# Channel mixing in pairs of feature blocks, with two PSUM banks read by one instruction

## The chip, the core and the metric

The kernel runs on one NeuronCore of a Trainium2 chip. Five engines with queues of their own work on it: TensorE (PE in the profile, its weight loads PEld), VectorE (DVE), ScalarE (ACT), GpSimd (POOL) and SyncE (SP). Each takes its instructions strictly in the order in which they were issued to it; an instruction that waits for a semaphore holds up all that stand behind it on its engine.

The metric is the time of one execution on the device in microseconds. Before the change the median of three runs is 2263.96 us.

## The reference

Eight batches of 4096 tokens with 192 channels go through an attention over seven taps and then through two matrix products over tokens and two over channels.

```python
# attention: a causal window of K = 7 rows, weights by head (8 heads of 24 channels)
w = softmax(weight_gen)                      # B, S, H, K
out = einsum('bshk,bskhg->bshg', w, x_unf)   # x_unf: the window's rows
# token mixing, d_tok = 256
h = maximum(xt @ w_tok1, 0) @ w_tok2         # xt: channels by tokens
u = x + h.T
# channel mixing, d_ch = 1536
h2 = maximum(u @ w_ch1, 0) @ w_ch2
result = u + h2
```

The products are to be as good as float32. [...]

## The kernel before

**Chunks and blocks.** A batch is cut into 8 chunks of 512 tokens, 64 chunks in all. The 1536 features of the channel mixing are 12 blocks of 128. The main loop (line 811) goes over the chunks `g` and within each over the blocks `f`. One step is `channel1(g, f)`, five matmuls of 512 columns into one PSUM bank `ph` (line 504), and behind it `channel2` for the block two before (`LAG = 2`): eight matmuls, four of 384 columns (line 520) and four of 192 (line 522), which add up in the four banks `acc`.

**From `ph` to `h`.** When a `ph` is complete, ScalarE writes `relu(ph)`, rounded, as the hi part of `h` (line 507), and after that VectorE writes `relu(ph) - hi` as the lo part (line 508). Only then may the bank be written again. `ph` has a ring of two banks, `ps_h`, so that block `f + 2` waits on TensorE for the lo part of block `f`.

**Between the blocks.** Three kinds of work for other chunks stand between the steps of a chunk. `token1` (eight matmuls of 384 and eight of 192 columns into `th`, lines 397 and 398) is the first token product of a chunk up to nine chunks ahead; VectorE adds what it leaves to `h1s` (lines 406 and 408). `token2_half`, called twice, is the second token product of chunk `g + 1` (into `up`, lines 452 and 453); ScalarE copies its right-hand part to `q2` (line 461), VectorE adds the left-hand part to the attention's result (line 463) and later `q2` to that (line 472). `th` and `up` share a ring of their own, one tile of two banks (`ps_m`). [...]

**The columns of the next chunk.** `channel1` of chunk `g + 1` needs `u` with the channels on the partitions, in two parts. `columns_of` makes them once both halves of `token2` are done: VectorE transposes blocks of 32 by 32 (line 476, tile `t`), ScalarE moves 24 pieces of 32x128 to their partitions (line 484, tiles `a_f` and `c_f`), then it casts `a_hi` and the upper half of `uc` (lines 424 and 425), and VectorE takes the differences `a_lo` and the lower half of `uc` (lines 426 and 429). The first matmul of a step reads `a_hi`, the third `a_lo`, the fourth and the fifth `uc`.

**Attention.** VectorE computes the taps of a chunk eight to nine chunks ahead: seven multiplications (line 200) and six additions (line 208) of 128x768.

**Who sets the order.** The program is written by a planner in Python that runs when the kernel is built. It keeps an estimated time per engine (`at`), adds a cost for what it issues, and lets `pump(limit)` put waiting work (the attention, conversions, column moves) between the steps as long as VectorE would not be later than `limit`, which is `SLACK` past the time at which the next lo part can be taken. A column move is planned at 200 ns. On the chip only the resulting order is in force; the engines wait for semaphores, not for the plan.

**Leaving a chunk.** `store` (line 526) adds `acc` and `u`: VectorE the left-hand parts (line 534), ScalarE copies the right-hand parts to `q` (line 535), VectorE adds them (line 539), and GpSimd's queue issues the store (line 540).

**Stages.** Up to 130 us the first batch's attention and token mixing are done and the weights are converted. The token products take float32 values in the first two batches and split ones from the third on. In the last batch there is no attention and no `token1` left.

Of the kernel before, what the change touches and what calls it, by code (L numbers as in the profile page):

```python
# [21 lines left out]
def mixer_kernel(ctx: ExitStack, tc: tile.TileContext, x, wg, wt1, wt2, wc1, wc2, out):  # L22
# [11 lines left out]
    NF = F // P  # L34
    KR = R // P
# [34 lines left out]
    xt = {}  # L70

    def load_x(m):
        """Four rows on each partition, with the six rows before them."""
# [72 lines left out]
    def split(hi, lo, v):  # L146
        """The part of v that TensorE takes in one pass, and the rest."""
# [28 lines left out]
    def taps(src, wn, j, k0, k1):  # L176
        """The rows of taps k0..k1-1, and their weights along the channels of a head."""
# [38 lines left out]
    def two_parts(m):  # L216
        """For the token mixing, after the first batches."""
# [13 lines left out]
    # The first batch, before anything is there for TensorE to do: it adds up the taps.  # L231
# [35 lines left out]
    def load_w1(m):  # L267
        """The first batches take float32 values; for the next one they are split, once."""
# [40 lines left out]
    def load_w2(m):  # L309
        """The first batches take float32 values; for the next one they are split, once."""  # L310
# [122 lines left out]
    Q = 32                   # VectorE transposes blocks of so many rows and columns  # L433
    NQ = P // Q
    ur, q2 = {}, {}

    def token2_half(m, half):
        """Two of the four tokens of each partition."""
        b, i = divmod(m, NCH)
        xa, h1, w = xat[m], h1t[b], w2t[m]  # L440
        if m == 0 and half == 1:
            up = ps_acc.tile([P, 2, 512], F32, tag="acc0", name="up")
        else:
            up = ps_m.tile([P, 2, 512], F32, tag="m", name="up")
# [22 lines left out]
    def columns_of(m):  # L467
        """The same with the channels on the partitions: the blocks transposed, then each moved."""
        box = {}

        def add():
            nc.vector.tensor_add(ur[m], ur[m], q2.pop(m))

        def turn():
            t = late.tile([P, CT, D], F32, tag="q2", name="t")
# [10 lines left out]
        if m in q2:  # L486
            yield "v", 876, add
# [8 lines left out]
    ht, acc_t = {}, {}  # L496

    def channel1(g, f):
        a_hi, a_lo, uc = ut[g]
        ph = ps_h.tile([P, N], F32, tag="ph", name="ph")  # L500
        fs = slice(f * P, (f + 1) * P)
        steps = ((w1a_hi, a_hi), (w1a_lo, a_hi), (w1a_hi, a_lo), (w1c_hi, uc), (w1c_lo, uc))
        for n, (w, u) in enumerate(steps):
            nc.tensor.matmul(ph, w[:, fs], u, start=n == 0, stop=n == len(steps) - 1)  # L504
# [7 lines left out]
    def channel2(g, f):  # L512
# [10 lines left out]
        if f == NF - 1:  # L523
            ut.pop(g)
# [364 lines left out]
```

## Time and profile before

| | |
|---|---|
| median of three runs (lowest to highest) | 2263.96 us (2263.43 to 2265.24) |
| span of the profiled execution | 2262.6 us |
| instructions | 31755 |
| PE busy | 2173.1 us, 96% |
| DVE busy | 1846.8 us, 82% |
| ACT busy | 1253.6 us, 55% |
| POOL busy | 58.5 us, 3% |
| HBM traffic over the span | 107 GB/s |

The span runs from the first instruction to the last. Busy times are unions of an engine's instructions. A matmul's duration in the trace reaches past the start of the next one, because matmuls are pipelined; what TensorE really takes for one is read from start to start. The same holds, by a smaller amount, for VectorE. The profiled execution's span lies 1.4 us under the median of the runs.

### The profile page before, as it was taken

To read this page: it belongs to the slowest core of one execution; us is meant where nothing else is said; L and a number is where in the kernel's file an instruction comes from. 1 tells how busy PE (TensorE), PEld (TensorE's weight loads), DVE (VectorE), ACT (ScalarE), POOL (GpSimd) and SP (SyncE) were. 2 spreads that over 40 slices of the span, in tenths; PEclk is the share of its full clock that TensorE was granted. 3 is DMA by queue.
4 is the path that set the end of the run, shared out by engine and by line. 5 is a ranking of instruction groups with operands and counts; after the bars stand their busy time and mean duration, and the time that the engine had idled before them with its cause. 6 is when DMAs were issued, how large, how long until landed. Compare 5 with 4: busy or idle time off the path is not lost.

```text
span 2262.6 us, 31755 instructions
## 1 busy us (share of the span) xinstructions
PE 2173.1 (96%) x12256; PEld 1946.5 (86%) x12256; DVE 1846.8 (82%) x2504; ACT 1253.6 (55%) x2873; POOL 58.5 (3%) x104
## 2 busy tenths in 40 slices
PE   7969999999999999999999999999999999999997
PEld 5658889999889889889888888888888898888987
DVE  8978889999888889788888888888888888644443
ACT  4686553655565555555556455555545555555553
POOL 0000000000000000000000000000000000000000
PEclk9989999999999999999999999999999999999999
DMA  7734122333323333223323322322332331111100
GB/s 277 244 131 146 65 100 82 121 128 116 111 113 124 117 123 137 102 92 128 110 84 124 128 95 99 128 105 85 128 128 87 107 124 70 64 52 52 52 33 15
DMA packets 52136, 244.75 MB, mean 108 GB/s; under 512 B 6008, under 2 KB 15736, under 8 KB 38672
## 3 DMA queue, kind: packets, MB, share of 16 engines
q1 hardware_dynamic: 43360, 196.58, 24.8%
q0 software_dynamic: 8624, 46.14, 5.0%
q8 instruction: 96, 1.57, 0.3%
q14 instruction: 56, 0.46, 0.1%
HBM read 192.36 MB, written 50.33 MB: 107 GB/s over the span
## 4 chain that ended last, share of the span: by engine, by line
PE 36%; issue 31%; ACT 18%; DVE 13%; DMA 1%; POOL 1%; SPq 0%; POOLq 0%; ACTq 0%; DVEq 0%
PE ph L504 15%; ACT a_f L484 8%; PE acc L520 8%; ACT h L507 4%; PE acc L522 4%; ACT c_f L484 3%; DVE h L508 3%; PE th L397 2%; PE up L452 2%; PE tapsum L251 2%; PE up L450 2%; DVE pr L200 2%; DVE xa L208 2%; PE th L398 1%; DVE prk L240 1%
## 5 line engine op out<-in xcount | busy, mean ns | idle before, releaser
L520 PE MATMUL acc<-w2s,h 128*128 128x384 f32 x3072 | 914.1, 354 | 2.8 <-ACT q L535 2.7
L507 ACT ACTIVATE h<-ph 128x512 fp32r<-128x512 f32 x768 | 458.0, 597 | 661.5 <-PE ph L504 616.4
L522 PE MATMUL acc<-w2s,h 128*128 128x192 f32 x3072 | 770.4, 251 | 0.0
L508 DVE SCALAR_TENSOR_TENSOR h<-ph,h 128x512 fp32r<-128x512 f32 x768 | 527.2, 686 | 297.3 <-ACT h L507 293.6
L522 PEld LDWEIGHTS acc<-w2s,h 128*128 128x128 f32 x3072 | 584.8, 190 | 29.8
L520 PEld LDWEIGHTS acc<-w2s,h 128*128 128x128 f32 x3072 | 577.0, 188 | 37.3 <-ACT q L535 4.8
L504 PE MATMUL ph<-a_hi,w1a_hi 128*128 128x512 f32 x768 | 333.2, 434 | 49.2 <-DVE h L508 38.9
L208 DVE TENSOR_TENSOR xa<-xa,pr 128x768 f32<-128x768 f32 x336 | 319.2, 950 | 0.3
L200 DVE TENSOR_TENSOR pr<-xt,wn 128x768 f32<-128x768 f32 x336 | 317.1, 950 | 2.4
L484 ACT COPY a_f<-t 32x128 f32<-32x128 f32 x1024 | 302.7, 296 | 17.6 <-DVE t L476 5.2
L504 PE MATMUL ph<-uc,w1c_hi 128*128 128x512 f32 x768 | 302.5, 394 | 2.2 <-DVE uc L429 2.2
L504 PE MATMUL ph<-a_lo,w1a_hi 128*128 128x512 f32 x768 | 303.8, 396 | 0.0
L504 PE MATMUL ph<-a_hi,w1a_lo 128*128 128x512 f32 x768 | 302.6, 394 | 0.0
L504 PE MATMUL ph<-uc,w1c_lo 128*128 128x512 f32 x768 | 299.0, 389 | 0.0
L504 PEld LDWEIGHTS ph<-a_hi,w1a_hi 128*128 128x128 f32 x768 | 144.5, 188 | 72.7 <-DVE h L508 61.0
L504 PEld LDWEIGHTS ph<-uc,w1c_hi 128*128 128x128 f32 x768 | 144.5, 188 | 36.6 <-DVE uc L429 3.2
L504 PEld LDWEIGHTS ph<-uc,w1c_lo 128*128 128x128 f32 x768 | 144.6, 188 | 34.2
L504 PEld LDWEIGHTS ph<-a_lo,w1a_hi 128*128 128x128 f32 x768 | 144.6, 188 | 32.9 <-DVE a_lo L426 0.8
L484 ACT COPY c_f<-t 32x128 f32<-32x128 f32 x512 | 152.2, 297 | 7.1
L504 PEld LDWEIGHTS ph<-a_hi,w1a_lo 128*128 128x128 f32 x768 | 147.0, 191 | 0.1
L452 PE MATMUL up<-h,w 128*128 128x384 f32 x384 | 118.4, 364 | 3.6 <-PE acc L522 3.1
L397 PE MATMUL th<-xh,w 128*128 128x384 f32 x384 | 112.9, 359 | 0.0
(72 smaller groups left out, 2026.1 us busy)
## 6 DMA issues: line engine op xcount, KB each, us to landing
w<-s SPq DMA_DIRECT2D x80, 1024.0 KB
xt<-in_x_dram SPq DMA_DIRECT2D x56, 960.0 KB
out_dram<-o POOLq DMA_DIRECT2D x63, 384.0 KB, 3.1
raw<-in_moe_w_tok_dram SPq DMA_DIRECT2D x16, 1024.0 KB
s<-w POOLq DMA_DIRECT2D x16, 1024.0 KB, 4.2
val<-s SPq DMA_DIRECT2D x24, 512.0 KB
wg<-in_weight_gen_dram SPq DMA_DIRECT2D x64, 112.0 KB
s<-val SPq DMA_DIRECT2D x8, 512.0 KB
```

The source lines that it names most:

```text
L200: nc.vector.tensor_mul(dst.rearrange("p t (h g) -> p (t h) g", h=H).rearrange("p (o n) g -> p o n g", o=1), x_k, w)
L208: nc.vector.tensor_add(box["acc"], box["acc"], box.pop(k))
L251: nc.tensor.matmul(ps[:, n, 0:half * D], ident, prs[k][:, n * half:(n + 1) * half, :], start=k == 0, stop=k == K - 1)
L397: nc.tensor.matmul(th[:, r, 0:2 * D], w[:, c, 0, rs], xh[:, c, :], start=c == 0, stop=False)
L450: nc.tensor.matmul(up[:, j, 0:D], w[:, k, cs], h1[:, k, :], start=k == 0, stop=k == KR - 1)
L452: nc.tensor.matmul(up[:, j, 0:2 * D], w[:, k, 0, cs], h1[:, k, :], start=k == 0, stop=False)
L484: nc.scalar.copy(dst[to:to + Q, :].rearrange("p (c n j) -> p c n j", c=CT, n=NQ)[:, :, n, :], box["t"][n * Q:(n + 1) * Q, :, d, :])
L504: nc.tensor.matmul(ph, w[:, fs], u, start=n == 0, stop=n == len(steps) - 1)
L507: nc.scalar.activation(h[:, 0], ph, AF.Relu)
L508: nc.vector.scalar_tensor_tensor(h[:, 1], ph, 0.0, h[:, 0].bitcast(F32), op0=ALU.max, op1=ALU.subtract)
L520: nc.tensor.matmul(ps[:, 0:2 * D], h[:, 0, cs], w2s[:, f, :], start=f == 0, stop=False, **kw)
L522: nc.tensor.matmul(ps[:, 0:D], h[:, 1, cs], w2s[:, f, 0:D], start=False, stop=f == NF - 1, **kw)
```

## The change

- The 12 blocks of a chunk become 6 pairs (`NP`). `channel1(g, p)` runs the ten matmuls of two blocks into a tile of two banks; one instruction of ScalarE and one of VectorE then read both banks (128x2x512 elements) for the hi and the lo parts. `h` holds a pair and has three buffers instead of four single ones.
- `channel2(g, p)` takes a pair, sixteen matmuls, and runs two pairs behind.
- `ps_h` and `ps_m` are replaced by `ps_w`: two tiles of two banks each, which pairs and token products take in turn, in the order of the program.
- The right-hand parts of `up` and of `acc` are no longer copied by ScalarE: VectorE adds them from PSUM, each with one more instruction. `store` adds into `ur` (three buffers) and stores from there; `o`, `q` and `q2` go.
- The planner's costs and rules follow: `C1, C2 = 2290, 2264` for the two products of a pair, `TOP, LOW = 1040, 1135` for the two reads, `LATE = 300`, `FIRST = 0`, one queue `w_at` for the times at which the two tiles come free. The cost of a column move stays 200.

```diff
-    ps_h = ctx.enter_context(tc.tile_pool(name="ps_h", bufs=2, space=bass.MemoryType.PSUM))
-    ps_m = ctx.enter_context(tc.tile_pool(name="ps_m", bufs=1, space=bass.MemoryType.PSUM))
+    ps_w = ctx.enter_context(tc.tile_pool(name="ps_w", bufs=2, space=bass.MemoryType.PSUM))
...
-        th = ps_m.tile([P, 2, 512], F32, tag="m", name="th")
+        th = ps_w.tile([P, 2, 512], F32, tag="w", name="th")
...
+        up = ps_w.tile([P, 2, 512], F32, tag="w", name="up")
...
-            ur[m] = late.tile([P, CT, D], F32, tag="ur", name="ur", bufs=2)
+            ur[m] = late.tile([P, CT, D], F32, tag="ur", name="ur", bufs=3)
+        u = ur[m][:, ts, :]
+        nc.vector.tensor_add(u, up[:, :, 0:D], xa[:, ts, :])
         if b >= F2:
-            if half == 0:
-                q2[m] = late.tile([P, CT, D], F32, tag="q2", name="q2")
-            nc.scalar.copy(q2[m][:, ts, :], up[:, :, D:2 * D])
-        yield
-        nc.vector.tensor_add(ur[m][:, ts, :], up[:, :, 0:D], xa[:, ts, :])
+            nc.vector.tensor_add(u, up[:, :, D:2 * D], u)
...
-    def channel1(g, f):
+    def channel1(g, p):
         a_hi, a_lo, uc = ut[g]
-        ph = ps_h.tile([P, N], F32, tag="ph", name="ph")
-        fs = slice(f * P, (f + 1) * P)
+        ph = ps_w.tile([P, 2, 512], F32, tag="w", name="ph")
         steps = ((w1a_hi, a_hi), (w1a_lo, a_hi), (w1a_hi, a_lo), (w1c_hi, uc), (w1c_lo, uc))
-        for n, (w, u) in enumerate(steps):
-            nc.tensor.matmul(ph, w[:, fs], u, start=n == 0, stop=n == len(steps) - 1)
-        h = late.tile([P, 2, N], F32R, tag="h", name="h", bufs=4)
-        ht[g, f] = h
-        nc.scalar.activation(h[:, 0], ph, AF.Relu)
+        for j in range(2):
+            fs = slice((2 * p + j) * P, (2 * p + j + 1) * P)
+            for n, (w, u) in enumerate(steps):
+                nc.tensor.matmul(ph[:, j, :], w[:, fs], u, start=n == 0, stop=n == len(steps) - 1)
+        h = late.tile([P, 2, 2, N], F32R, tag="h", name="h", bufs=3)
+        ht[g, p] = h
+        nc.scalar.activation(h[:, :, 0, :], ph, AF.Relu)
         nc.vector.scalar_tensor_tensor(
-            h[:, 1], ph, 0.0, h[:, 0].bitcast(F32), op0=ALU.max, op1=ALU.subtract
+            h[:, :, 1, :], ph, 0.0, h[:, :, 0, :].bitcast(F32), op0=ALU.max, op1=ALU.subtract
         )
...
     def store(g):
...
-        for n in range(2):
-            nc.vector.tensor_add(o[:, ts[n], :], a[n][:, :, 0:D], u[:, ts[n], :])
-            nc.scalar.copy(q[:, ts[1 - n], :], a[1 - n][:, :, D:2 * D])
...
+        for n, a in enumerate(acc_t.pop(g)):
+            t = slice(2 * n, 2 * n + 2)
+            for l in range(2):
+                nc.vector.tensor_add(u[:, t, :], a[:, :, l * D:(l + 1) * D], u[:, t, :])
...
-    LATE = 200               # ScalarE for the copies of h
-    FIRST = 1                # the block of features from which on the next chunk's token mixing may come
-    h_at, ph_at, h1_at = {}, [0.0, 0.0], {0: 0.0}
+    LATE = 300
+    FIRST = 0
+    C1, C2 = 2290, 2264
+    TOP, LOW = 1040, 1135
+    h_at, w_at, h1_at = {}, deque([0.0, 0.0]), {0: 0.0}
...
-                    end = max(at["pe"], ph_at[0]) + 1080 + LATE
+                    end = max(at["pe"], w_at[0]) + C1 + LATE
```

**How the order moves.** Before, a chunk in the middle of the run is on TensorE: blocks 0 and 1, `token1`, block 2, the first half of `token2`, block 3, the second half, blocks 4 to 11. After, it is pair 0, first half, pair 1, `token1`, pair 2, second half, pairs 3, 4 and 5. Each block or pair stands here for both its products.

On ScalarE, the columns of the next chunk in the middle of a chunk before, from the reads of blocks 4 and 5 (line 507 is the hi part, line 484 a column move):

```order
L507 ACTIVATE h<-ph 128x512 x2
L484 COPY a_f<-t 32x4x32 x8
L507 ACTIVATE h<-ph 128x512
L484 COPY a_f<-t 32x4x32 x8
L507 ACTIVATE h<-ph 128x512
L484 COPY c_f<-t 32x4x32 x8
L507 ACTIVATE h<-ph 128x512
L424 CAST a_hi<-a_f 128x512
L425 CAST uc<-c_f 64x512
L507 ACTIVATE h<-ph 128x512 x5
```

The same place after, from the reads of pairs 2 and 3 (line 499 is the hi part of a pair, line 476 a column move):

```order
L499 ACTIVATE h<-ph 128x2x512 x2
L476 COPY a_f<-t 32x4x32 x16
L476 COPY c_f<-t 32x4x32 x2
L499 ACTIVATE h<-ph 128x2x512
L476 COPY c_f<-t 32x4x32 x6
L424 CAST a_hi<-a_f 128x512
L425 CAST uc<-c_f 64x512
L499 ACTIVATE h<-ph 128x2x512 x3
```

Where eight moves stood between two reads, eighteen stand now, and six more with both casts behind the read of pair 4.

On VectorE, the end of a chunk before, from the lo part of block 8 to that of block 11 (line 508; `a_lo` and `uc` are the next chunk's):

```order
L508 SCALAR_TENSOR_TENSOR h<-ph,h 128x512
L426 TENSOR_TENSOR a_lo<-a_f,a_hi 128x512
L200 TENSOR_TENSOR pr<-xt,wn 128x768
L429 TENSOR_TENSOR uc<-c_f,uc 64x512
L508 SCALAR_TENSOR_TENSOR h<-ph,h 128x512
L208 TENSOR_TENSOR xa<-xa,pr 128x768
L508 SCALAR_TENSOR_TENSOR h<-ph,h 128x512
L200 TENSOR_TENSOR pr<-xt,wn 128x768
L208 TENSOR_TENSOR xa<-xa,pr 128x768
L508 SCALAR_TENSOR_TENSOR h<-ph,h 128x512
```

After, from the lo part of pair 4 (line 500) over that of pair 5 to that of pair 0 of the next chunk:

```order
L500 SCALAR_TENSOR_TENSOR h<-ph,h 128x2x512
L200 TENSOR_TENSOR pr<-xt,wn 128x768
L426 TENSOR_TENSOR a_lo<-a_f,a_hi 128x512
L208 TENSOR_TENSOR xa<-xa,pr 128x768
L429 TENSOR_TENSOR uc<-c_f,uc 64x512
L500 SCALAR_TENSOR_TENSOR h<-ph,h 128x2x512
L200 TENSOR_TENSOR pr<-xt,wn 128x768
L208 TENSOR_TENSOR xa<-xa,pr 128x768
L200 TENSOR_TENSOR pr<-xt,wn 128x768
L208 TENSOR_TENSOR xa<-xa,pr 128x768
L500 SCALAR_TENSOR_TENSOR h<-ph,h 128x2x512
```

Up to four instructions of 128x768 or smaller stand between two lo parts now, where one to two stood.

Chunk 5 and the last chunks of the second to the sixth batch (15, 23, 31, 39 and 47) now carry two `token1`, behind pairs 0 and 1, and the halves of `token2` behind pairs 2 and 3. The chunks 16, 24, 32, 40 and 48 carry no `token1` and have the halves behind pairs 0 and 1, as the chunks from 56 on have.

More of the change, by code (lines that the diff above doesn't have):

```diff
@@ L34, in mixer_kernel @@
     NF = F // P
+    NP = NF // 2
     KR = R // P
@@ L469, in columns_of @@
         box = {}
-        def add():
-            nc.vector.tensor_add(ur[m], ur[m], q2.pop(m))
         def turn():
-            t = late.tile([P, CT, D], F32, tag="q2", name="t")
+            t = late.tile([P, CT, D], F32, tag="t", name="t")
             nc.vector.transpose(t.rearrange("p c d -> p (c d)"), ur[m].rearrange("p c d -> p (c d)"))
@@ L555, in mixer_kernel @@
     SLACK_M = 400
-    LATE = 200
-    FIRST = 1
-    h_at, ph_at, h1_at = {}, [0.0, 0.0], {0: 0.0}
-    free = {"acc": 0.0, "m": 0.0, "u": 0.0}
+    LATE = 300
[3 more added lines that the diff above has]
+    h_at, w_at, h1_at = {}, deque([0.0, 0.0]), {0: 0.0}
+    free = {"acc": 0.0, "u": 0.0}
     ready = deque()
@@ L776, in do_token1 @@
         next(it)
-        end = on("pe", 2160 if m >= F1 * NCH else 2600, t, free["m"])
+        end = on("pe", 2264 if m >= F1 * NCH else 2600, t, w_at.popleft())
         state["token1"] = m
@@ L780, in do_token1 @@
         next(it, None)
-        free["m"] = on("dve", 1000 if m >= F1 * NCH else 500, end)
+        w_at.append(on("dve", 1000 if m >= F1 * NCH else 500, end))
         if m % NCH == NCH - 1:
-            h1_at[m // NCH] = on("act", 420, free["m"])
+            h1_at[m // NCH] = on("act", 420, w_at[-1])
             if m >= F2 * NCH:
@@ L813, in mixer_kernel @@
         state["rush"] = g == 0
-        for f in range(NF if g < NG else LAG):
+        for p in range(NP if g < NG else LAG):
             if g == 0:
-                need(lambda: f * P < HF or ("w1a", 1) in done)
-            if g == 0 and f >= LAG:
-                need(lambda: ("c2", (f - LAG) // NF2) in done)
+                need(lambda: (2 * p + 2) * P <= HF or ("w1a", 1) in done)
+            if g == 0 and p >= LAG:
+                need(lambda: ("c2", 2 * (p - LAG) // NF2) in done)
             if g < NG:
-                channel1(g, f)
-                end = on("pe", 1080, ph_at.pop(0), free["u"] if f == 0 else 0.0)
-                end = on("act", 480, end)
-                h_at[g, f] = on("dve", 602, end)
-                ph_at.append(h_at[g, f])
-            n = g * NF + f - LAG
+                channel1(g, p)
+                end = on("pe", C1, w_at.popleft(), free["u"] if p == 0 else 0.0)
+                end = on("act", TOP, end)
+                h_at[g, p] = on("dve", LOW, end)
+                w_at.append(h_at[g, p])
+            n = g * NP + p - LAG
             if n >= 0:
-                prev = divmod(n, NF)
+                prev = divmod(n, NP)
                 channel2(*prev)
-                on("pe", 1080, h_at.pop(prev))
-                if prev[1] == 0:
-                    on("pe", 0, free["acc"])
-            if f == LAG - 1 and g > 0:
-                items = store(g - 1)
-                item = next(items)
-                end = on("act", 740, at["pe"] + HOP)
-                free["acc"] = max(end, on("dve", 940, at["pe"] + HOP))
-                chains.append(Chain(chain([item], items)))
+                on("pe", C2, h_at.pop(prev), free["acc"] if prev[1] == 0 else 0.0)
+            if p == LAG - 1 and g > 0:
+                store(g - 1)
+                free["acc"] = on("dve", 2000, at["pe"] + HOP) - 570
             pump(next_lo() + (SLACK if g > NCH else SLACK0))
-            if token1_ready() and (f == LAG - 1 or ready[0][0] < g + NCH + ((g + 1) % NCH == 0)):
+            if token1_ready() and (p == LAG - 1 or ready[0][0] < g + NCH + ((g + 1) % NCH == 0)):
                 do_token1()
@@ L842, in mixer_kernel @@
                 next(parts, None)
-            elif f >= FIRST and g + 1 in w2t and (g + 1) // NCH in h1t \
-                    and max(free["m"], h1_at[(g + 1) // NCH]) <= at["pe"]:
+            elif p >= FIRST and g + 1 in w2t and (g + 1) // NCH in h1t \
+                    and max(w_at[0], h1_at[(g + 1) // NCH]) <= at["pe"]:
                 parts = do_token2(g + 1)
```

58 lines of the change are left out of this document (22 added, 36 removed).

## The prediction

> **What bounds the kernel now.** I read the page first (shares, slices, groups), then the waits, then a table of windows cut where chunks begin, then the timelines of TensorE, ScalarE and VectorE around one chunk. The table holds `channel1`'s matmuls (line 504) alone; 60 of them are a chunk, 480 are eight. Its first columns are the window, its length and TensorE's busy time.
>
> ```profile
> PE 2173.1 (96%) x12256; PEld 1946.5 (86%) x12256; DVE 1846.8 (82%) x2504; ACT 1253.6 (55%) x2873; POOL 58.5 (3%) x104
> 170.90:413.10 242.20, 116.09 (x421) 1.00 0.29 102
> 413.10:679.30 266.20, 131.04 (x480) 1.00 0.31 116
> 679.30:950.50 271.20, 130.97 (x480) 0.99 0.33 118
> 950.50:1215.00 264.50, 129.37 (x480) 1.00 0.30 109
> 1215.00:1479.80 264.80, 129.35 (x480) 1.00 0.31 109
> 1479.80:1744.70 264.90, 129.31 (x480) 1.00 0.30 109
> 1744.70:2008.80 264.10, 129.37 (x480) 1.00 0.25 88
> 2008.80:2221.20 212.40, 112.75 (x421) 1.00 0.12 44
> ```
>
> A chunk takes 33.1 us in the middle and 30.3 in the last batch. What TensorE would need without waits comes from starts (block, `token1`, block, half of `token2`, block):
>
> ```profile
> 1515.42 0.41 PE L504 MATMUL ph<-a_hi,w1a_hi 128*128 128x512 f32 x1
> 1516.59 0.33 PE L520 MATMUL acc<-w2s,h 128*128 128x384 f32 x1
> 1517.70 0.36 PE L397 MATMUL th<-xh,w 128*128 128x384 f32 x1
> 1519.98 0.42 PE L504 MATMUL ph<-a_hi,w1a_hi 128*128 128x512 f32 x1
> 1522.25 0.36 PE L452 MATMUL up<-h,w 128*128 128x384 f32 x1
> 1523.39 0.41 PE L504 MATMUL ph<-a_hi,w1a_hi 128*128 128x512 f32 x1
> ```
>
> A block takes 1.17 + 1.11 = 2.28 us, `token1` 2.28, a half 1.14. Twelve blocks and the token products make 31.92. So a middle chunk loses 1.1 us, and 48 chunks from 413.1 to 2008.8 lose 1595.7 - 48 x 31.92 = 63.5. The waits say to what: TensorE stands before a new `ph` until VectorE has taken the lo part, and never long for the next chunk's columns.
>
> ```profile
> PEld ph L504 <- DVE h L508: 61.0, 96, 6.6
> 1507.03 0.69 DVE L508 SCALAR_TENSOR_TENSOR h<-ph,h 128x512 fp32r<-128x512 f32 x1 [0.68 <-ACT h L507]
> 1507.78 0.50 PE L504 MATMUL ph<-a_hi,w1a_hi 128*128 128x512 f32 x1 [0.38 <-DVE h L508]
> 1508.11 0.40 PE L504 MATMUL ph<-a_hi,w1a_lo 128*128 128x512 f32 x1
> ```
>
> TensorE starts 0.06 us after the lo part ends, and its first step after a wait takes 0.33 instead of 0.25. VectorE had itself waited for ScalarE, which is late because of column moves:
>
> ```profile
> 1516.79 0.60 ACT L507 ACTIVATE h<-ph 128x512 fp32r<-128x512 f32 x1 [1.69 <-PE ph L504]
> 1533.49 0.60 ACT L507 ACTIVATE h<-ph 128x512 fp32r<-128x512 f32 x1
> 1534.11 2.44 ACT L484 COPY a_f<-t 32x128 f32<-32x128 f32 x8
> 1539.69 0.60 ACT L507 ACTIVATE h<-ph 128x512 fp32r<-128x512 f32 x1
> 1540.31 0.62 ACT L424 CAST a_hi<-a_f 128x512 fp32r<-128x512 f32 x1
> 1540.84 0.61 ACT L425 CAST uc<-c_f 64x512 fp32r<-64x512 f32 x1
> ```
>
> ScalarE reads 0.20 after TensorE turns to the next product (1516.59, 1516.79). Eight moves take 2.47 with the gap behind them, 0.309 each, where the plan counts 0.20. A move follows a read by 0.62.
>
> **The change part by part.** TensorE's work stays: the same matmuls in another order.
>
> *The two wide reads.* Nothing before reads 1024 elements of PSUM; these rows bound it:
>
> ```profile
> L507 ACT ACTIVATE h<-ph 128x512 fp32r<-128x512 f32 x768 | 458.0, 597 | 661.5 <-PE ph L504 616.4 <-DVE h L508 37.4 <-DVE xa L208 3.4
> L508 DVE SCALAR_TENSOR_TENSOR h<-ph,h 128x512 fp32r<-128x512 f32 x768 | 527.2, 686 | 297.3 <-ACT h L507 293.6
> L424 ACT CAST a_hi<-a_f 128x512 fp32r<-128x512 f32 x64 | 39.7, 620 | 1.5
> L426 DVE TENSOR_TENSOR a_lo<-a_f,a_hi 128x512 fp32r<-128x512 f32 x64 | 44.1, 688 | 2.8 <-ACT a_hi L424 2.8
> L149 ACT CAST w<-val 128x1024 fp32r<-128x1024 f32 x16 | 16.7, 1045 | 0.2
> L150 DVE TENSOR_TENSOR w<-val,w 128x1024 fp32r<-128x1024 f32 x16 | 19.4, 1213 | 1.1 <-ACT w L149 1.1
> L476 DVE STREAM_TRANSPOSE t<-ur 128x768 f32<-128x768 f32 x64 | 62.1, 971 | 0.5
> ```
>
> From 512 to 1024 elements a cast grows by 425 ns and a difference by 525. So I take 597 + 450 = 1.05 us for the hi part (1.0 to 1.19, twice the narrow one) and 686 + 530 = 1.22 for the lo part (1.15 to 1.37). The tile is free 0.20 + 1.05 + 0.03 + 1.22 + 0.06 = 2.56 us after the pair's last matmul at best.
>
> VectorE is busy 82% and idles 297 us before line 508, all for ScalarE; ScalarE is busy 55%. Neither is saturated. [...]
>
> *The copies that go to VectorE.* Per chunk four copies of 128x384 leave ScalarE. VectorE gets eight additions of 128x384 for four such and two of 128x768: the same elements in two more instructions. A narrow lo part holds VectorE 0.61 (below), 0.53 of it for its 512 elements, so each costs some 0.1. It hides where VectorE idles; without that cover it is 0.2 a chunk, inside the bounds below.
>
> *The ring.* Order on TensorE after: pair 0, half, pair 1, `token1`, pair 2, half, pairs 3, 4, 5. Two tiles are taken in turn, so pair 1 takes pair 0's tile after only one second product and a half, 2.22 + 1.14 = 3.36 us; against 2.56 that leaves 0.8. Pair 3 takes pair 2's on the same terms; the others have 4.5 to 6.8.
>
> *The columns.* Set 0 where the second half's matmuls end. Before, eight blocks followed to the next chunk, 18.2 us; now three pairs, 13.68. Nothing gets shorter for it: still 24 moves, now with 18 in one run ahead of pair 4's read. VectorE's rows:
>
> ```profile
> 1048.77 0.95 DVE L208 TENSOR_TENSOR xa<-xa,pr 128x768 f32<-128x768 f32 x1
> 1049.76 0.96 DVE L200 TENSOR_TENSOR pr<-xt,wn 128x768 f32<-128x768 f32 x1
> 1050.63 0.68 DVE L508 SCALAR_TENSOR_TENSOR h<-ph,h 128x512 fp32r<-128x512 f32 x1
> 1540.96 0.69 DVE L426 TENSOR_TENSOR a_lo<-a_f,a_hi 128x512 fp32r<-128x512 f32 x1
> 1541.57 0.95 DVE L200 TENSOR_TENSOR pr<-xt,wn 128x768 f32<-128x768 f32 x1
> 1542.56 0.69 DVE L429 TENSOR_TENSOR uc<-c_f,uc 64x512 fp32r<-64x512 f32 x1
> 1543.27 0.69 DVE L508 SCALAR_TENSOR_TENSOR h<-ph,h 128x512 fp32r<-128x512 f32 x1
> 1543.88 0.95 DVE L208 TENSOR_TENSOR xa<-xa,pr 128x768 f32<-128x768 f32 x1
> ```
>
> From start to start: `xa` to `pr` 0.99, `pr` to the next 0.87 (I take that for `xa` to a lo part too), `a_lo` 0.61, an attention instruction to `uc` 0.99, `uc` 0.71, a lo part 0.61, so a wide one 0.61 + 0.53 = 1.13.
>
> ScalarE: read of pair 3 at 2.34 + 0.20 = 2.54; moves from 2.54 + 0.62 + 0.45 = 3.61 (two additions and the transpose, at most 0.2 + 0.87 + 0.87 + 0.97, are done by then); 18 x 0.309 later, at 9.17, the read of pair 4, whose matmuls were done at 6.90; six moves from 10.24; `a_hi` 12.09 to 12.71, `uc` to 13.23; read of pair 5.
>
> VectorE: lo of pair 4 at 9.17 + 1.05 + 0.03 = 10.25; `pr` 11.38; `a_lo` waits for `a_hi`, 12.74; `xa` 13.35; `uc` 14.34 to 15.03; lo of pair 5 at 15.05; `pr`, `xa`, `pr`, `xa` from 16.18; lo of the next pair 0 at 19.78 to 21.00; pair 1 may start at 21.06.
>
> TensorE: the next pair 0 at 13.68; its fourth matmul, 0.70 later, waits for `uc` until 15.09, 0.7 lost. Pair 1 would come at 13.68 + 4.56 + 1.14 = 19.38 without waits. It comes at 21.06: **1.7 us lost per regular chunk**. The rest of the chunk fits: counted from pair 1's start, VectorE is through its lo part at 4.8, `store`'s four additions at 6.9, `token1`'s two and a difference of 128x768 at 9.1 (some 2 more with a softmax); the lo part of pair 2 ends at 11.8 to 12.4, and pair 3 is due at 12.6. Period 33.6.
>
> *Batch ends.* Where the halves stand behind pairs 2 and 3, two pairs are left, 9.12 us. `a_hi` is done at 12.71, so pair 0 waits 3.65, then `uc` until 15.09 costs 1.54, with the restart 5.3. Before, such chunks lost no more than others: the rows of all four late batches lie at 264.1 to 264.9. The chunk after has its halves behind pairs 0 and 1, but its moves behind pair 3: chain and end both lie a pair later, and an `Exp` of some 0.5 stands in the chain, so the chunk that follows it loses 1.7 + 0.5 = 2.2. The double `token1` chunk itself loses 0.7 + 0.1 alone, because `token1` stands between its pairs 0 and 1.
>
> *The sum* from 413.1 to 2008.8: 32 regular chunks x 1.7 = 54.4; five batch ends x 5.3 = 26.5; five x 2.2 = 11; six x 0.8 = 4.8; 96.7 together. Of the 63.5 lost before, 8 stay: the second and third batch's rows are 1.7 and 6.5 above their neighbours, for float32 products and the splitting of weights. So 96.7 - 55.5 = +41. In the last batch pair 1 follows at 3.36 without attention in VectorE's queue, and columns have four pairs, 18.2: no waits, 6 x 4.56 + 2.28 = 29.64 against 212.4 / 7 = 30.34, -5 in seven chunks. Chunks 1 to 7 lose 11 of their 242.2 to conversions; I leave that at 0 (one early batch end against smoother pairs, -8 to +8). The span becomes 2262.6 + 41 - 5 = 2298.6. The runs' median lies 1.4 above the span: **2300**.
>
> Both wide reads at their cheap ends shorten the chain by some 0.3 on ScalarE and 0.3 on VectorE: 32 x 0.6 + 5 x 0.5 = 22 less, 2278. At the dear ends (+0.28 and +0.45): 27 more, 2327.
>
> **The rivals.** *Faster.* The chain from the second half to pair 1 is short enough and pairs remove the waits. It decides at 19.38: the chain must lose 1.7 of 21.06. If moves in a long run went at the planned 0.20, it would lose 24 x 0.109 = 2.6; regular waits would vanish and batch ends cost 2.7 each. Then 63.5 - 8 - 5 x 2.7 - 5 x 1 = 37 are won, with the 5 of the last batch 42: 2222. For it: fewer, larger instructions and a ring that gives most pairs 4.5 us or more. Against it: the measured 0.309, in every run of eight. 0.17.
>
> *No change.* My two losses overlap with slack that I don't see (VectorE's waits are counted one behind the other), and the 41 shrink to 5: 2264. 0.08.
>
> *The wide reads save nothing*, the change doesn't do what it says: each costs two narrow ones, 2327. 0.07.
>
> **How the numbers follow.** The forecast, 2275 to 2322, has 0.68. Faster by over 0.2% (4.5 us, about what a measurement of this kernel can tell) has 0.17, within 0.2% 0.08, slower 0.68 + 0.07 = 0.75. The range, 2258 to 2323, takes in the forecast, no change and the near edge of the faster case, and leaves out the rest of that and the dear reads.
>
> **What would show it.** Right: waits of `ph` for `uc`, and at batch ends for `a_hi`, which were nearly absent; one wait of about 1 us per chunk at pair 1 for pair 0's lo part; a middle batch near 272; the last batch's chunks at 29.7; hi parts at about 1.05 and lo parts at 1.22. Wrong: middle chunks at 32 to 32.5, or TensorE waiting elsewhere, above all at pair 3.

## The result, and the profile after

The changed kernel takes 2344.62 us, median of 4 runs (2343.15 to 2346.27), beside 2264.6 (2263.43 to 2265.95) for the kernel before on the same chip: a ratio of 1.0353, 95% interval 1.0339 to 1.0368. It is slower, as forecast, but by 80 us in place of 36, outside the range. The profiled execution has a span of 2342.1 us (before 2262.6) and a mean granted clock of 0.978 (before 0.993).

The page of after: the engines' busy time and the two wide reads (busy time, mean ns, idle time ahead and its releaser).

```profile
PE 2196.7 (94%) x12256; PEld 1962.0 (84%) x12256; DVE 1842.1 (79%) x2231; ACT 1085.0 (46%) x2265; POOL 58.4 (2%) x104
L499 ACT ACTIVATE h<-ph 128x1024 fp32r<-128x1024 f32 x384 | 392.8, 1023 | 1004.4 <-PE ph L496 980.3
L500 DVE SCALAR_TENSOR_TENSOR h<-ph,h 128x1024 fp32r<-128x1024 f32 x384 | 468.3, 1220 | 294.3 <-ACT h L499 292.7
```

The wide reads take 1023 and 1220 ns (forecast 1.05 and 1.22 us). VectorE idles for ScalarE as long as before (292.7 us, 293.6 before); ScalarE is freer than before (46% busy, 55% before). Neither engine got busier, and yet TensorE waits.

The windows of after, cut at chunks 1, 8, 16, 24, 32, 40, 48, 56 and 63 as those of before were, with `channel1`'s matmuls (line 496; columns: window, length, TensorE's busy time with them, granted clock, DMA share, GB/s):

```profile
167.40:425.80 258.40, 111.53 (x421) 0.97 0.28 99
425.80:720.10 294.30, 127.00 (x481) 0.98 0.29 107
720.10:1006.90 286.80, 128.44 (x481) 0.96 0.31 112
1006.90:1279.90 273.00, 123.59 (x480) 0.99 0.30 106
1279.90:1553.00 273.10, 123.65 (x481) 0.99 0.30 106
1553.00:1826.10 273.10, 123.67 (x480) 0.99 0.30 106
1826.10:2092.50 266.40, 123.43 (x481) 0.99 0.23 83
2092.50:2299.50 207.00, 103.39 (x421) 1.00 0.12 45
```

Against before, row by row: +16.2, +28.1, +15.6, +8.5, +8.3, +8.2, +2.3, -5.4. The middle batches came close to the forecast (255.36 + 5 x 1.7 + 0.8 + 5.3 + 2.2 = 272.2 by its terms), and so did the last one (207.0 / 7 = 29.57 a chunk, forecast 29.64). The first three rows did not.

What TensorE waited for (us in all, times, longest), two lines of before, then after:

```profile
PE ph L504 <- DVE h L508: 38.9, 77, 6.3
PE ph L504 <- DVE uc L429: 2.2, 2, 1.1
PE ph L496 <- DVE uc L429: 44.2, 54, 2.3
PE ph L496 <- ACT a_hi L424: 33.9, 12, 9.7
PE ph L496 <- DVE h L500: 24.6, 28, 7.0
PE ph L496 <- DVE a_lo L426: 6.0, 3, 3.2
```

The wait for the lo part of `h` shrank; waits for the next chunk's columns (`uc`, `a_hi`, `a_lo`) took its place (one wait of 9.7 us for `a_hi`, ahead of chunk 1, is in both kernels). Parts of the timeline of after at the end of a regular late chunk:

```profile
1447.50 0.41 PE L496 MATMUL ph<-a_hi,w1a_hi 128*128 128x512 f32 x1
1447.92 0.69 DVE L429 TENSOR_TENSOR uc<-c_f,uc 64x512 fp32r<-64x512 f32 x1
1448.65 0.50 PE L496 MATMUL ph<-uc,w1c_hi 128*128 128x512 f32 x1 [0.27 <-DVE uc L429]
1453.37 1.22 DVE L500 SCALAR_TENSOR_TENSOR h<-ph,h 128x1024 fp32r<-128x1024 f32 x1
1454.64 0.50 PE L496 MATMUL ph<-a_hi,w1a_hi 128*128 128x512 f32 x1 [0.73 <-DVE h L500]
```

With pair 0 at 13.68 on the prediction's scale, `uc` ends at 13.68 + (1447.92 + 0.69 - 1447.50) = 14.79 (forecast 15.03) and pair 0's lo part at 20.77 (forecast 21.00). Pair 1 starts 0.05 us behind it, after a wait. That chain was right.

The same place in an early chunk (10), where the weights of `token1` are still being split:

```profile
525.38 1.05 ACT L149 CAST w<-val 128x1024 fp32r<-128x1024 f32 x1
526.34 1.02 ACT L499 ACTIVATE h<-ph 128x1024 fp32r<-128x1024 f32 x1
526.47 1.22 DVE L150 TENSOR_TENSOR w<-val,w 128x1024 fp32r<-128x1024 f32 x1 [1.89 <-ACT w L149]
531.37 1.22 DVE L500 SCALAR_TENSOR_TENSOR h<-ph,h 128x1024 fp32r<-128x1024 f32 x1
532.61 0.69 DVE L429 TENSOR_TENSOR uc<-c_f,uc 64x512 fp32r<-64x512 f32 x1
```

The cast of a weight stands ahead of pair 4's read on ScalarE, and VectorE waits 1.89 us for it with everything that is queued behind. `uc` comes only after pair 5's lo part (531.37), and the next chunk's fourth matmul waits 2.3 us for it.

### The profile page after: what moved, and what is told of

Its sections match the earlier page's. It is cut to its first block, busy times and chain, and to the rows that moved or that the text cites. A ratio compares the mean times of both kernels' runs of the same rounds, so it can differ in the third digit from the quotient of the medians.

```text
span 2342.1 us, 30675 instructions
## 1 busy us (share of the span) xinstructions
PE 2196.7 (94%) x12256; PEld 1962.0 (84%) x12256; DVE 1842.1 (79%) x2231; ACT 1085.0 (46%) x2265; POOL 58.4 (2%) x104
## 4 chain that ended last, share of the span: by engine, by line
PE 38%; ACT 19%; DVE 14%; issue 11%; DMA 1%; POOL 0%; POOLq 0%; ACTq 0%; SPq 0%; DVEq 0%
PE ph L496 17%; ACT a_f L476 9%; PE acc L514 9%; ACT c_f L476 4%; PE acc L516 4%; ACT h L499 4%; DVE h L500 3%; DVE xa L208 3%; PE th L397 3%; DVE pr L200 3%; PE up L449 2%; DVE uc L429 1%; PE th L398 1%; DVE a_lo L426 1%; DMA w<-s 1%
## 5 line engine op out<-in xcount | busy, mean ns | idle before, releaser
L514 PE MATMUL acc<-w2s,h 128*128 128x384 f32 x3072 | 902.1, 358 | 0.0
L499 ACT ACTIVATE h<-ph 128x1024 fp32r<-128x1024 f32 x384 | 392.8, 1023 | 1004.4 <-PE ph L496 980.3
L500 DVE SCALAR_TENSOR_TENSOR h<-ph,h 128x1024 fp32r<-128x1024 f32 x384 | 468.3, 1220 | 294.3 <-ACT h L499 292.7
L516 PEld LDWEIGHTS acc<-w2s,h 128*128 128x128 f32 x3072 | 591.3, 192 | 16.0
L514 PEld LDWEIGHTS acc<-w2s,h 128*128 128x128 f32 x3072 | 583.3, 190 | 16.0
L496 PE MATMUL ph<-a_hi,w1a_hi 128*128 128x512 f32 x768 | 321.6, 419 | 58.9 <-ACT a_hi L424 33.9
L496 PE MATMUL ph<-uc,w1c_hi 128*128 128x512 f32 x768 | 311.7, 406 | 44.2 <-DVE uc L429 44.2
L496 PE MATMUL ph<-a_lo,w1a_hi 128*128 128x512 f32 x768 | 306.8, 399 | 6.0 <-DVE a_lo L426 6.0
L496 PE MATMUL ph<-uc,w1c_lo 128*128 128x512 f32 x768 | 305.2, 397 | 0.0
L528 DVE TENSOR_TENSOR ur<-acc,ur 128x384 f32<-128x384 f32 x256 | 136.2, 553 | 8.3 <-PE acc L516 3.9
```

The lines of the kernel that those rows point to most:

```text
L496: nc.tensor.matmul(ph[:, j, :], w[:, fs], u, start=n == 0, stop=n == len(steps) - 1)
L499: nc.scalar.activation(h[:, :, 0, :], ph, AF.Relu)
L500: nc.vector.scalar_tensor_tensor(h[:, :, 1, :], ph, 0.0, h[:, :, 0, :].bitcast(F32), op0=ALU.max, op1=ALU.subtract)
L514: nc.tensor.matmul(ps[:, 0:2 * D], h[:, j, 0, cs], w2s[:, f, :], start=f == 0, stop=False, **kw)
L516: nc.tensor.matmul(ps[:, 0:D], h[:, j, 1, cs], w2s[:, f, 0:D], start=False, stop=f == NF - 1, **kw)
L528: nc.vector.tensor_add(u[:, t, :], a[:, :, l * D:(l + 1) * D], u[:, t, :])
```

## The experiments

The table gives the median, the ratio to the kernel before in the same comparison with its interval, and the length of chunks 32 to 39 (start of `channel1` to start, in the profiled execution), where no weight is converted any more. Tight would be 8 x 31.92 = 255.4.

| kernel | us | ratio (95%) | chunks 32-39 |
|---|---|---|---|
| before | 2264.6 | 1 | 264.8 |
| changed | 2344.62 | 1.0353 (1.0339-1.0368) | 273.1 |
| before, halves three blocks later | 2381.78 | 1.0517 (1.0502-1.0533) | 276.1 |
| changed, halves behind pairs 0, 1 | 2324.48 | 1.0264 (1.0247-1.0281) | 273.2 |
| changed, moves planned at 310 | 2413.48 | 1.0651 (1.0635-1.0667) | 286.7 |
| both | 2225.35 | 0.9825 (0.9810-0.9840) | 255.0 |
| changed, splits held back | 2332.59 | 1.0298 (1.0283-1.0314) | 273.4 |
| changed, 8 moves on GpSimd | 2319.58 | 1.0232 (1.0215-1.0249) | 265.9 |
| both, narrow reads in turns | 2439.93 | 1.0760 (1.0742-1.0778) | 279.6 |
| both, narrow reads | 2225.94 | 0.9831 (0.9817-0.9846) | 255.1 |
| before, parts added by VectorE | 2279.80 | 1.0067 (1.0052-1.0082) | 265.5 |
| before, moves planned at 310 | 2314.68 | 1.0212 (1.0195-1.0229) | 276.3 |
| both, 310 from chunk 9 on | 2221.75 | 0.9806 (0.9792-0.9821) | 255.0 |
| both, 310 from chunk 8 on | 2213.27 | 0.9772 (0.9758-0.9787) | 255.1 |

**The halves later, in the kernel before.**

```diff
-    FIRST = 1
+    FIRST = 4
```

> The kernel before with the one number FIRST at 4 in place of 1: one block at a time, narrow reads, its own PSUM pools and ScalarE's copies as they were, but the halves of the second token product stand three blocks later, so that six blocks, 13.7 us, are left for the columns, as in the changed kernel. Theory: this alone makes it slower, by about 1 us and more in each regular chunk and by a lost clock behind long waits: 2310 us (2290 to 2345). Rivals 1 and 2 (ring, wide reads; VectorE's adds): nothing that they name is in this kernel, so it stays near 2264 (2255 to 2275).

Measured 2381.78: slower than the changed kernel, with none of its wide reads, none of its ring and none of its new additions. TensorE's waits:

```profile
PE ph L504 <- DVE uc L429: 58.4, 59, 1.9
PE ph L504 <- DVE h L508: 34.2, 57, 7.4
PE ph L504 <- ACT a_hi L424: 27.6, 10, 9.7
```

The wait for `uc`, 2.2 us in the kernel before, is 58.4. So a late second half alone makes such a loss. I expected at most 2345; chunks 16 to 23 alone took 308.0 in place of 271.2, and the mean granted clock fell to 0.977. Why it costs more here than in the changed kernel is not shown.

**The halves earlier, in the changed kernel.**

```diff
-            if token1_ready() and (p == LAG - 1 or ...
+            if token1_ready() and (p == LAG or ...
```

> The changed kernel with one condition of its order altered: in a regular chunk the halves of the second token product stand behind pairs 0 and 1 and the first token product behind pair 2 (it stood behind pair 1, the halves behind pairs 0 and 2). Theory (the columns no longer fit): the second half ends a pair and a token product earlier, so about 18 us are left for adds, transpose, moves and casts in place of 13.7, and uc is there before pair 0. A regular chunk of the late batches falls from 33.44 us to 31.9 to 32.2; at the batch ends the halves still stand behind late pairs, so the wait for a_hi stays. 42 regular chunks by about 1.4 give 2285 us (2265 to 2300). Rival 1 (the shared ring and the wide reads hold TensorE up): the same tiles are read in the same time, so the chunk stays within 0.3 us of 33.4, the time at 2330 to 2345. Rival 2 (VectorE has too much to do since it adds the right-hand parts): VectorE's work is the same, 2330 to 2345 too.

(`token1` then stands behind pair 2.) Measured 2324.48, a gain of 20 us where I expected 60 and outside my range; the late regular chunks took 32.3 to 34.6 us, no less on average than before the edit. TensorE's waits in chunks 32 to 39, beside one of 3.2 for `a_hi` at the batch end:

```profile
PE ph L496 <- DVE h L500: 7.8, 5, 2.3
PE ph L496 <- DVE uc L429: 1.5, 2, 0.9
```

VectorE's timeline around the end of chunk 33 and the start of 34, with TensorE's pair 1:

```profile
1319.45 0.96 DVE L225 TENSOR_TENSOR xh<-xa,xh 128x768 fp32r<-128x768 f32 x1 [1.85 <-ACT xh L222]
1333.79 1.22 DVE L500 SCALAR_TENSOR_TENSOR h<-ph,h 128x1024 fp32r<-128x1024 f32 x1
1335.06 0.50 PE L496 MATMUL ph<-a_hi,w1a_hi 128*128 128x512 f32 x1 [1.65 <-DVE h L500]
```

The columns are in time now. But 18 moves stand ahead of the cast `xh` on ScalarE, planned at 3.6 us and lasting 5.5; VectorE waits 1.85 for it. Behind that, its attention work, placed by a plan that knows of no delay, puts pair 0's lo part late, and pair 1 waits for the tile. The position alone does not do it.

**The moves at their real price; and both.**

```diff
-            yield "u", 200 * len(part), lambda part=part: move(part)
+            yield "u", 310 * len(part), lambda part=part: move(part)
```

> The changed kernel with the moves planned at 310 ns each and the order of the steps as the change has it (halves behind pairs 0 and 2). The planner then ends the columns of a regular chunk behind the last pair's read: two moves, the cast to a_hi and the cast to uc stand between the reads of pair 5 and of the next pair 0. Theory (13.7 us do not hold the columns, at whatever price): the wait stays, at pair 0 in place of pair 1, 33.6 to 34 us for a regular chunk, 2345 us (2315 to 2375). Rival 3 (the price alone was wrong, the order is good): regular chunks at 31.9 to 32.3, the time at 2220 to 2270.

> As a_swap, and the moves of the columns are planned at 310 ns each, about what they take in one run, in place of 200. Then the planner puts 18 of them before one read of h and 6 and the casts before the next, and by the order of instructions the batch ends come out like regular chunks: no chunk with two first token products ahead of its halves. Theory: all late chunks at 31.9 to 32.2 us, batches 24 to 31 and on at 256 to 258 us in place of 273, the early chunks better by some 60 us in all: 2215 us (2200 to 2240), under the kernel before. Rival 1 (ring and wide reads): within 15 us of the changed kernel, 2330 to 2345. Rival 2 (VectorE): the same 2330 to 2345.

The price alone gives 2413.48, worse by 69 and by more than I expected. The casts now stand behind the last pair's read, and TensorE waits for them (of this kernel):

```profile
PE ph L496 <- DVE uc L429: 56.7, 56, 1.1
PE ph L496 <- ACT a_hi L424: 54.2, 56, 9.7
```

The position alone gives -20, both together -119: 2225.35, under the kernel before. The windows of the version with both, chunks 1 to 15 and 24 to 39:

```profile
169.00:439.80 270.80, 117.24 (x421) 0.95 0.28 100
439.80:702.50 262.70, 123.23 (x480) 0.98 0.32 114
957.70:1212.70 255.00, 118.40 (x480) 1.00 0.32 113
1212.70:1467.70 255.00, 118.45 (x480) 1.00 0.32 114
```

From chunk 17 to 54 each chunk takes 31.88, the tight value, with the clock at 1.00 and the wide reads, the ring and VectorE's additions all in place. So none of these by itself holds TensorE up. At a chunk end of this version:

```profile
1334.92 0.68 DVE L429 TENSOR_TENSOR uc<-c_f,uc 64x512 fp32r<-64x512 f32 x1
1338.18 1.03 ACT L499 ACTIVATE h<-ph 128x1024 fp32r<-128x1024 f32 x1 [3.52 <-PE ph L496]
```

`uc` is complete before pair 5's matmuls are, a whole pair ahead of its use.

**The splits held back.**

```diff
-        yield "a", 190 + n * 0.75, lambda: nc.scalar.copy(hi, v)
+        yield kind, 190 + n * 0.75, lambda: nc.scalar.copy(hi, v)
```

(`kind` is "s" for both token weights.)

> The changed kernel with the first step of the splits of both token weights planned as work of ScalarE by itself, which is held back while moves of a chunk's columns wait. It touches chunks 1 to 23 alone. Theory (conversions and splits stand in the columns' chain in those chunks): chunks 8 to 15 fall from 294 us towards 277 and chunks 16 to 23 from 287 towards 279, the late batches stay at 273; 2318 us (2308 to 2332). Rival 1 and rival 2: the early chunks lose by the ring or by VectorE's load, which are the same, so 2338 to 2348.

2332.59, just outside what I expected. Chunks 8 to 14 fall from 248.6 to 237.1 (425.6 to 662.7 below), 33.9 each:

```profile
425.60:662.70 237.10, 107.56 (x420) 1.00 0.28 102
```

The weight's cast now stands behind that to `uc`:

```profile
525.78 0.61 ACT L425 CAST uc<-c_f 64x512 fp32r<-64x512 f32 x1
526.30 1.05 ACT L149 CAST w<-val 128x1024 fp32r<-128x1024 f32 x1
```

But chunks 15 (46.2, 45.7 in the changed kernel) and 16 to 23 (286.1, 286.8) stay. Over the run TensorE now waits 7.0 us for weights of `token1` that come late, 3.1 before this edit.

**Eight moves on GpSimd.**

```diff
-                nc.scalar.copy(dst[...], box["t"][...])
+                copy = nc.scalar.copy if d < NQ else nc.gpsimd.tensor_copy
+                copy(dst[...], box["t"][...])
```

> The changed kernel with the 8 of 24 moves that fill c_f on GpSimd, which is idle, in place of ScalarE; every other instruction stays where it was, since the plan is not told. Theory (the end of the columns' chain on ScalarE sets the wait): ScalarE is done 2.5 us earlier, and if GpSimd's copies are no slower than twice ScalarE's 0.3 us the regular chunk falls from 33.44 us to about 32: 2280 us (2260 to 2310). If GpSimd needs over 1 us for one, uc comes later still and it is slower than 2344. Rival 1 (ring and wide reads) and rival 2 (VectorE's adds): the chunk stays at 33.4 whatever ScalarE is spared, 2335 to 2345.

GpSimd takes 570 ns for a move, ScalarE 295 in the changed kernel. The group of its moves:

```profile
L477 POOL COPY c_f<-t 32x128 f32<-32x128 f32 x512 | 292.0, 570 | 432.4 <-DVE t L468 413.8
```

GpSimd's timeline in an early chunk:

```profile
485.97 0.54 POOL L281 DMA_DIRECT2D s<-w  x1 [7.28 <-DVE w L150]
486.56 3.59 POOL L477 COPY c_f<-t 32x128 f32<-32x128 f32 x6
```

With ScalarE relieved, a regular chunk of 32 to 39 takes 32.4 in place of 33.4, and the eight take 265.9 in place of 273.1: the end of the columns' chain sets much of the wait. The total is 2319.58, 40 over my value, since in the early chunks six of a chunk's moves stand on GpSimd behind a DMA issue that waits 7.28 us for the split `w`; chunks 8 to 14 take 263.2.

**Narrow reads, twice.** In the version with both edits, each bank of a pair is read by its own instruction; first in turns (ScalarE, VectorE, ScalarE, VectorE), then with both of ScalarE's ahead:

```diff
-        nc.scalar.activation(h[:, :, 0, :], ph, AF.Relu)
+        for j in range(2):
+            nc.scalar.activation(h[:, j, 0, :], ph[:, j, :], AF.Relu)
...
```

> The fastest version so far (halves behind pairs 0 and 1, moves at 310) with narrow reads: each bank of a pair is read by an instruction of its own on ScalarE and on VectorE, as in the kernel before; order and plan are otherwise the same. Theory: TensorE sets the time in all chunks from 9 on and both readers have room, so the two narrow reads, 1.19 us in place of 1.02 on ScalarE and 1.37 in place of 1.22 on VectorE, cost next to nothing: 2225 us (2220 to 2240). Rival 4 (the wide reads are what makes this version fast): a pair's reads last 0.15 us longer on VectorE in each of 384 pairs and its queue runs late, 2250 us and more.

> The version with halves behind pairs 0 and 1 and moves at 310 (2225.35 us), again with narrow reads, but now both of ScalarE's reads of a pair are issued ahead of VectorE's two, so that ScalarE's second does not stand behind VectorE's first, as it did in the narrow version that took 2439.93 us. Theory: that version lost by its order, not by the width of the reads; with 1.19 us in place of 1.02 on ScalarE and 1.37 in place of 1.22 on VectorE the queues stay nearly on time: 2235 us (2225 to 2265). Rival 4 (the wide reads are what makes it fast, 0.15 us of VectorE in each pair): VectorE's queue runs late by 0.9 us a chunk, pair 1 waits for pair 0's tile in every chunk, 2280 us and more.

In turns: 2439.93 (2435.01 to 2440.90, and one run of 4207.79). Not narrowness did that, but the order. The groups of reads of the version in turns: ScalarE's wait 687.9 us for VectorE's lo parts, VectorE's 422.6 for ScalarE's:

```profile
L500 ACT ACTIVATE h<-ph 128x512 fp32r<-128x512 f32 x768 | 449.1, 596 | 1198.6 <-DVE h L501 687.9 <-PE ph L496 510.0
L501 DVE SCALAR_TENSOR_TENSOR h<-ph,h 128x512 fp32r<-128x512 f32 x768 | 528.5, 688 | 424.6 <-ACT h L500 422.6
```

With both of ScalarE's reads ahead, ScalarE waits for TensorE, and the time is that of the wide reads, 2225.94 against 2225.35; the same groups:

```profile
L500 ACT ACTIVATE h<-ph 128x512 fp32r<-128x512 f32 x768 | 417.0, 595 | 989.8 <-PE ph L496 923.7 <-issue 65.3
L502 DVE SCALAR_TENSOR_TENSOR h<-ph,h 128x512 fp32r<-128x512 f32 x768 | 493.2, 684 | 281.7 <-ACT h L500 280.8
```

My expectation for the first was wrong by 215 us, because I had not seen that my edit also changed the order; that for the second fell on its low end. The wide reads save busy time (1.02 and 1.22 us against 1.19 and 1.37) and, in this version, no time.

**VectorE's additions alone, in the kernel before.**

```diff
-            nc.scalar.copy(q2[m][:, ts, :], up[:, :, D:2 * D])
...
+            nc.vector.tensor_add(u, up[:, :, D:2 * D], u)
```

> The kernel before with one part of the change alone: the right-hand parts of the second token product are added by VectorE from PSUM, two adds of 0.55 us in each half, and ScalarE's two copies and VectorE's wide add go. Theory: VectorE has about 0.2 us more in a chunk of some 33 and the halves stay behind the same blocks, so no difference of size: 2264 us (2250 to 2285). Rival 2 (VectorE has too much to do since it adds the right-hand parts): slower than 2290.

(The plan's costs follow.) 2279.80, 15 slower, within the range that I gave but not the 2264. The run does not price the additions alone, because the order moved too: chunk 1 starts at 175.0 in place of 170.9, and in the first batch, ahead of it, no such addition stands. Chunks 32 to 39 lose 0.7 (265.5 for 264.8), the last batch's 3.8. So the additions cost a fifth of the loss at most in this kernel; in the version with both edits no cost shows.

**The price alone, in the kernel before.** The same edit of the price.

> The kernel before with its moves planned at 310 in place of 200. Theory: there 18 us are left and the columns end five blocks ahead of the next chunk, so the low price did no harm; at 310 the planner spreads them four to a block, the casts come to stand around the next chunk's first block, and block 0 waits for uc: slower, 2295 us (2265 to 2330). Rival 3 (the low price is what holds every version up): the kernel before gains as well, 2225 to 2255.

2314.68: slower. The right price does not help by itself; it helps where the place fits.

**The first chunks at the old price.**

```diff
-            yield "u", 310 * len(part), lambda part=part: move(part)
+            yield "u", (200 if m <= NCH else 310) * len(part), lambda part=part: move(part)
```

and then `m <= 7`, so that 310 holds from chunk 8 on.

> The fastest version so far with the moves at 310 from chunk 9 on only; up to chunk 8 they are planned at 200 as in the changed kernel. Theory: with 310 the first chunks lost their time to casts that stood behind the last pair's read; with 200 they stand ahead of it and chunks 1 to 7 fall from 271 us to about 259, the rest stays at 31.9 to 32.3 per chunk: 2213 us (2208 to 2222). Rival: the first chunks are bound by VectorE's conversions, whatever the casts do: 2222 to 2230.

> The version with halves behind pairs 0 and 1 and moves at 310, the moves of the first seven chunks at 200: as the one that kept 200 up to chunk 8 (2221.75 us), but by its order of instructions without two first token products in chunk 15, which cost that one about 10 us in chunks 15 and 16. Theory: chunks 1 to 7 near 259 us, chunk 8 near 37, 31.9 to 32.3 from chunk 9 on: 2214 us (2208 to 2222). Rival (what the first chunks save is given back later by another order of the attention's work): 2221 to 2228.

The first took 2221.75: chunks 1 to 7 fell to 259.0 as expected, but chunk 15 got its two `token1` back (38.9 for 31.9) and chunk 16 lost 3.4. The second took 2213.27, expected 2214, the fastest version: 2.3% under the kernel before. Its chunks 1 to 7 still take 258.7, 16 more than before's, so there is more to be had.

## Why the prediction was right in direction and wrong in size

- *TensorE's needs, prices of the reads, the columns' chain*: right. A regular late chunk takes 33.4 (forecast 33.6); `uc` and pair 0's lo part came within 0.25 us of the worked chain. The cheap end of the range was added up wrongly: the chain holds two reads of ScalarE and three of VectorE, so 2 x 0.05 + 3 x 0.07 = 0.31 could be saved, not 0.6, and the low value would have been about 2289 in place of 2278. That is not the side on which it failed.
- *VectorE's eight additions hidden*: borne out by the version that keeps them and runs tight. The 0.2 a chunk without cover is not tested by itself.
- *Batch ends*: the wait for `a_hi` is there, 3.2 us (forecast 3.65), but chunk 32 took 33.3, where 29.64 and the other 5.3 - 3.65 = 1.65 of a batch end make 31.3. The missing 2.0 are the clock, below: 6.8 us at 0.51 lose 3.3, and the wait for `uc`, 0.7 in place of 1.54, gives a part of it back. Regular chunks came 0.2 shorter; that the batch fits all the same is luck, two errors that cancel.
- *The last batch*: right, less the last chunk, which takes 1.8 longer (32.03 for 30.26). Two more blocks of second products come behind its last pair; I had not priced that. They are missing at the other end: chunk 1 starts 3.5 us earlier, at 167.4.
- **The step that failed** is the treatment of the early chunks: "of the 63.5 lost before, 8 stay" and "chunks 1 to 7 ... I leave that at 0". I took the conversions over at what they cost before, and I put the early batch end, the clock behind long waits and the loading of weights at nothing. By the prediction's own terms chunks 8 to 15 would have taken 8 x 31.92 + 2.28 (the second `token1`) + 7 x 1.7 + 0.8 + 3.65 + 1.7 = 275.7, and chunks 16 to 23 8 x 31.92 + 1.65 + 2.2 + 5 x 1.7 + 0.8 + 3.65 + 6.5 = 278.7; they took 294.3 and 286.8, and chunks 1 to 7 16.2 more than before. 18.6 + 8.1 + 16.2 = 42.9 of the 44 us missed. The trace says where they lie.
  - *Chunks 10 to 14*, 13 us above their terms. Before, the columns had 18.2 us and a weight's cast and difference, 1.05 and 1.22, could stand in their chain; in 13.7 they could not. Each of these chunks waits 2.3 us for `uc`, and three of the five lose 1.7 of clock behind that. This is shown by experiment: with the splits held back chunks 8 to 14 got 11.5 us back.
  - *Chunks 5 to 7*, all of the 16.2. Chunk 5 now carries the second `token1`, two chunks earlier than before, and that waits 3.9 us for its weights (1.1 before, in chunk 7); the batch end costs 4.0 for `a_hi`, and the `uc` of chunks 5 to 7 another 3.9; the granted clock is 0.94 from 306.8 to 425.8. Holding the splits back changed nothing here (46.3, 37.1 and 35.5 us).
  - *Chunks 15 to 18*, 19 us above their terms. TensorE waits there some 17 us for columns and weights, where the terms allow 10, and the granted clock is 0.92 from 674.4 to 831.3, with 1.00 in the same chunks before. That these columns come late is read from the waits; no run isolates why.

The waits of after in chunk 5 (the first line), in front of chunk 6 (the second), and from 720.1 to 1006.9 (the others):

```profile
PE th L415 <- DMA val<-s: 3.9, 1, 3.9
PE ph L496 <- ACT a_hi L424: 4.0, 1, 4.0
PE ph L496 <- ACT a_hi L424: 9.5, 4, 4.2
PE ph L496 <- DVE a_lo L426: 3.9, 2, 3.2
```

- *No price for the clock.* Between chunks 10 and 11 of after the instructions and the wait, 2.3 us for `uc`, are the same; one takes 36.7 us and the other 35.1. The windows behind the two waits, and behind a batch end's:

```profile
496.80:503.80 7.00, 7.00 (x32) 0.76 0.48 163
533.40:540.40 7.00, 6.96 (x39) 1.00 0.46 179
1279.90:1286.70 6.80, 6.11 (x16) 0.51 0.01 2
```

The seven us at 0.76 lose 7 x 0.24 = 1.7 us of clock, about the difference of the two chunks. Over the span, (1 - 0.978) x 2342.1 = 51.5 us of clock are missing, before (1 - 0.993) x 2262.6 = 15.8: at most 36 of the 80 us are clock, less where TensorE was waiting anyway. In chunks 5 to 18, fourteen times 3.41 us at half clock lose up to 24 us, of the 42.9 that the early chunks took beyond the forecast.

Behind which waits the clock fell can be read from the trace's record of it. In after every stretch at half clock (0.50) starts a whole number of 3.413 us from every other (behind the waits of chunks 10, 12 and 14 they start at 498.1, 569.8 and 641.5, 21 such steps apart). Laid over these steps, chunk 10's wait (494.5 to 496.8) has 2.1 us in one step; chunk 11's (531.1 to 533.4) is cut in two, 1.1 and 1.2. From the first such stretch to the end of the run all 16 steps at full clock with 1.6 us or more without a matmul were followed by half clock, and none of the 615 with 1.54 or less was. That is the count of one trace. In the kernel before with the halves three blocks later, where windows of 3 us were read, half clock from 1573.9 us on follows a step with 1.55 us at most, so that the border may lie lower there. What makes the clock fall is not shown.

- *The rivals.* "Faster" was to be decided by whether the chain could lose 1.7 us; the eight moves on GpSimd took more than that from ScalarE, and a regular late chunk lost 1.0 of its 1.5 us, chunks 32 to 39 7.2 of their 17.7. That the wide reads save nothing is so in the version with both edits, 2225.35 against 2225.94 with narrow reads, though each does cost less than two narrow ones. The changed kernel itself was not run with narrow reads.

The theory (the columns no longer fit) stands for the regular chunks, with one correction: place and price act together. The ring, the wide reads and VectorE's additions, as causes of the loss by themselves, are ruled out by the version that keeps all three and runs tight from chunk 17 on. For chunks 5 to 7 and 15 to 18 the causes are read from waits and clock, and not shown by a run.

## What to carry to other kernels

When an order shortens the time that a side chain has, price again everything that may stand inside that chain, the work of the first stages too, not only the chain in its steady state. A list scheduler's place for a step and its price for the work behind it are one setting: here the price alone lost 69 us, the place alone won 20, and both together won 119, from 3.5% slower than the kernel before to 1.7% faster. An edit that is meant to change one size can change the order across engines as well; look at who waits for whom before its time is read as the price of the size.

## What the runs showed of the hardware that was not expected

- A wait of TensorE could cost more than its length: behind 3.2 us at a batch end of after the granted clock stood at 0.51 for 6.8 us; behind 2.3 us it stood at 0.76 for 7.0 us in one chunk and at 1.00 in the next. In after's record of the clock all 16 steps of 3.413 us at full clock with 1.6 us and more without a matmul were followed by half clock, and none of the 615 with 1.54 or less.
- ScalarE's read of 1024 elements over two PSUM banks took 1023 ns against 2 x 595 for two reads of one bank each, VectorE's 1220 against 2 x 684 (wide in after, narrow in the version with both edits).
- GpSimd's 32x128 copy took 570 ns, ScalarE's 295.
